# Routed attention and a PReLU layer on one core: sums of a pair of heads in one product, inverses spread by one turn, checks by the batch, rows in other PSUM banks

## The chip, the cores and the metric

The kernel runs on one core of one Trainium2 chip. The metric is the device time of one execution in microseconds (us); a median of several runs is given. A core has the engines TensorE (PE; its weight loads are listed as PEld), VectorE (DVE), ScalarE (ACT), GpSimd (POOL) and SyncE (SP), each with a queue of its own; here SP, ACT and POOL issue DMA transfers.

## The reference

Two stages, one after the other. First, attention in which a query sees only the keys that were assigned to the same of 16 clusters:

```python
# q, k, v: (4, 8, 768, 64); centroids: (8, 16, 64)
q_assign = np.argmax(np.einsum('bhsd,hcd->bhsc', q_n, c_n), axis=-1)   # rows normed
k_assign = np.argmax(np.einsum('bhsd,hcd->bhsc', k_n, c_n), axis=-1)
mask = q_assign[:, :, :, None] == k_assign[:, :, None, :]
scores = np.where(mask, scale * np.matmul(q, k.transpose(0, 1, 3, 2)), -1000000000.0)
attn = np.exp(scores - np.max(scores, axis=-1, keepdims=True))
attn = attn / (np.sum(attn, axis=-1, keepdims=True) + 1e-09)
x = np.matmul(attn, v)                 # then (B,H,S,D) -> (B*S, H*D) = (3072, 512)
...
h = x @ w_in                           # w_in (512, 2048)
g = np.maximum(h, 0.0) + alpha * np.minimum(h, 0.0)
return (g @ w_out).astype(np.float32)  # w_out (2048, 512)
```

`w_in`, `w_out` and `alpha` come in as words of 64-bit floats and are turned into 32-bit ones on the way.

## The kernel before, in words

**Tiles and steps.** Heads are worked in pairs: 4 batches x 4 pairs give 16 pairs n = 0 to 15 (`pairs`, L104). For the first three batches (n < NO = 12) a pair's 768 queries go in two halves of 384 against all six key chunks of 128, three steps of two chunks each: 72 steps. I call these far blocks. The last batch (n = 12 to 15) is sorted: the tokens of each head are put into the order of their clusters in HBM (`order_*`, L472 to L682), so that a key chunk has to meet only its neighbours (`window`, L694). Such a near block also has three steps, 72 to 83 in all, and makes both halves ("sides") of a pair at once.

**What a block does.** `score` multiplies keys by queries and takes exp on ScalarE; `mask` zeroes (VectorE, L772) what belongs to another cluster; `add_up` or `add_near` adds the chunks for the denominators, `turn` transposes 32 x 32 blocks (L801), `rows_sums` reduces them (L807), `total` adds over partitions by a product with the constant `fold` (L817), `invert` takes reciprocals and spreads them over a 128 x 384 tile `rd` by transposes (L827, L832), `weigh` or `weigh_near` makes the products with v (L861, L897), and `normalise` multiplies them with `rd` (L965, L903). The first batch's first half sums by products with ones instead (L854 to L882). After each inverse, `check` (L326) takes the lowest and highest of its words for a flag that is read at the end.

**Last batch.** Its result has to go back to the old order. `normalise_near` writes `outT`; `to_rows` (L923) transposes three chunks at a time on TensorE into PSUM and ScalarE copies them (L930); `put_back` scatters rows to HBM by 12 indirect DMAs on POOL (L935); `fetch_back` loads them on SP (L947), and `turn_back` transposes them on VectorE into the FFN's input xT (L957).

**FFN.** `ffn_pieces` cuts the FFN of half a batch into 28 pieces: `hidden(f)` (8 matmul records, L989, a ScalarE copy, L995, and a VectorE operation for the slope a piece later, L981) and `final` (8 records, L1007; every second one ends with a copy or addition of y, L1013 and L1015, and the last with a store). They fill PE between the steps.

**The order is written out by hand.** From step 24 on, a block of three steps has 12 slots (2 + 5 + 5, counted here 0 to 11). In each slot, `tick` first runs what was put off (`later(k, ...)`: k ticks on), then one entry of `todo` (masks, additions, turn, sums, product), one of `sorting`, then `feed` lets a number of FFN pieces go, spread evenly over the 48 slots of four blocks; `kept(block)` says how many are held back at their end (10 for the last four blocks, whose pieces fill the tail while the rows return). Then come the preparations of later blocks (`prep_at`). In the tail (L1228) two ticks and one piece alternate. In near blocks the product of side 0 is entry 6 of `todo`, its inverse entry 7, the product of side 1 entry 11.

**Buffers in PSUM.** `ps_m` (tile `mps`, from `misc()`) has one buffer, used for cluster similarities, clusters, `total`, rows and the products of side 1 in near blocks. `ps_f` (tile `fps`) has two that go round, used for FFN pieces and for one chunk of each `score`. `ps_s` and `ps_v` hold scores and weighted sums.

Of the kernel before, what the change touches and what calls it, by code (L numbers as in the profile page):

```python
# [23 lines left out]
def kernel(  # L24
# [122 lines left out]
    alf = const.tile([NF, P], FP32, name="alf")  # L147
# [54 lines left out]
    cn = const.tile([P, D], FP32, name="cn")  # L202
# [119 lines left out]
    lowest = const.tile([P, 2 * NP], FP32, name="lowest")  # L322
    highest = const.tile([P, 2 * NP], FP32, name="highest")
    WORDS = [float((127 + e) * 2 ** 23) for e in (-50, 40)]

    def check(n, half, inverses):  # L326
        i = 2 * n + half
        for to, op in ((lowest, ALU.min), (highest, ALU.max)):
            nc.vector.tensor_reduce(out=to[:, i:i + 1], in_=inverses.bitcast(I32), axis=AX.X,
                                    op=op)  # L330
# [157 lines left out]
    def order_constants():  # L488
        ordc = sorts["ordc"]
        stage = [ordc.tile([P, NX // PARTS, P], FP32, name=f"stage{i}") for i in range(STAGES)]  # L490
        for t in stage:
            nc.gpsimd.memset(t, 0.0)
# [9 lines left out]
        brief = asg.tile([P, HS], FP32, name="simT")  # L502
        for i, pattern in enumerate(kinds):
            row = (ordc.tile([P, P], FP32, name=f"row{i}") if i else brief[:, 0:P])
            nc.gpsimd.iota(row, pattern=pattern, base=0, channel_multiplier=0,
                           allow_small_or_imprecise_dtypes=True)
            own = brief[:, P:2 * P]
            nc.gpsimd.tensor_tensor(out=own, in0=row, in1=ident, op=ALU.mult)
            nc.vector.tensor_reduce(out=cols[:, i:i + 1], in_=own, axis=AX.X, op=ALU.add)
            rows.append(row)  # L510
        same = brief[:, 2 * P:3 * P]
        nc.vector.tensor_scalar(out=same, in0=rows[1], scalar1=cols[:, 1:2], scalar2=None,
                                op0=ALU.is_equal)


        before, within = rows[1], rows[2]
        nc.vector.scalar_tensor_tensor(out=before, in0=rows[0], scalar=cols[:, 0:1],
                                       in1=same, op0=ALU.is_gt, op1=ALU.mult)
        nc.vector.scalar_tensor_tensor(out=same, in0=rows[0], scalar=cols[:, 0:1],
                                       in1=same, op0=ALU.is_equal, op1=ALU.mult)  # L520
        nc.vector.scalar_tensor_tensor(out=within, in0=rows[2], scalar=cols[:, 2:3],
                                       in1=same, op0=ALU.is_gt, op1=ALU.mult)
        nc.vector.tensor_tensor(out=within, in0=within, in1=before, op=ALU.add)


        shift = ordc.tile([P, 2], FP32, name="shift")
        nc.vector.tensor_scalar(out=shift[:, 0:1], in0=cols[:, 2:3], scalar1=-float(HS),
                                scalar2=None, op0=ALU.mult)
        nc.vector.tensor_scalar(out=shift[:, 1:2], in0=cols[:, 1:2], scalar1=2.0,
                                scalar2=float(S), op0=ALU.is_ge, op1=ALU.mult)  # L530
        nc.vector.tensor_scalar(out=shift[:, 1:2], in0=shift[:, 1:2], scalar1=-1.0,
                                scalar2=None, op0=ALU.add)
# [20 lines left out]
    def order_counts(n, ps):  # L553
# [11 lines left out]
        for i, piece in enumerate(pieces):  # L565
            later(i, piece) if i else piece()
# [238 lines left out]
    def rows_sums(n, half):  # L805
        part = rdp.tile([P, 2 * NX], FP32, name="part")
        nc.vector.tensor_reduce(out=part, in_=accTs.pop((n, half)), axis=AX.X, op=ALU.add)  # L807
        parts[n, half] = part
# [4 lines left out]
    def total(n, half):  # L813

        if (n, half) in parts:
            ps = misc()
            nc.tensor.matmul(out=ps[:, 0:2 * NX], lhsT=fold, rhs=parts.pop((n, half)),  # L817
                             start=True, stop=True)
            totals[n, half] = ps

    def invert(n, half):

        if (n, half) not in totals:
            return
        ps = totals.pop((n, half))
        inv = rdp.tile([P, 2 * NX], FP32, name="inv")
        nc.vector.reciprocal(out=inv, in_=ps[:, 0:2 * NX])  # L827
        pool = sorts["ordp"] if n >= NO and half else rdp
        rd = pool.tile([P, HS], FP32, name="rd")
        for h in range(2):  # L830
            r = slice(h * D, (h + 1) * D)
            nc.vector.transpose(  # L832
                out=rd[r, :],
                in_=inv[r, h * NX:(h + 1) * NX, None].broadcast_to((D, NX, Q)))
        rds[n, half] = rd
        check(n, half, inv)

    def weigh(m, denominators=False):
# [24 lines left out]
        if denominators and done:  # L863
# [6 lines left out]
            inv = rdp.tile([P, 2 * NX], FP32, name="inv")  # L870
# [5 lines left out]
            for h in range(2):  # L876
                nc.vector.tensor_copy(out=inv[h * D + Q:(h + 1) * D, 0:NX],
                                      in_=inv[h * D:h * D + Q, 0:NX])
            rd = rdp.tile([P, HS], FP32, name="rd")
            nc.vector.transpose(out=rd, in_=inv[:, 0:NX, None].broadcast_to((P, NX, Q)))  # L880
            rds[n, half] = rd
            later(1, lambda: check(n, half, inv[:, 0:NX]))  # L882
# [17 lines left out]
    def normalise_near(n):  # L900
# [13 lines left out]

        starts = (4, 6) if n == NP - 1 else (6, 10)
# [7 lines left out]
    def to_rows(outT, rows, i):  # L923

        ps = misc()
# [521 lines left out]
```

## Time and profile before

| | |
|---|---|
| median of 3 runs | 1000.96 us (1000.15 to 1003.37) |
| the profiled execution | 1003.53 us, span 1001.4 us |
| granted TensorE clock | 0.995 of full speed |
| PE busy | 968.5 us, 97% of the span |
| DVE, ACT, POOL busy | 650.4, 259.6, 211.8 us |
| L989, L1007 (FFN products) | 342.9 and 339.2 us of PE |
| L772 (masks) / L832 (spreading inverses) / L329 (checks) | 131 us / 32.1 us (56 of 573 ns) / 10.9 us (64 instructions) |

The profile is one execution on the chip. Busy times overlap between engines. A wait is put down to the instruction that released it; times of a timeline row are its start and its duration, with the idle time of its engine before it in brackets. Matmul ends are modelled, and the next one may start 0.17 us before the end shown of the one ahead of it.

### The profile page before, as it was taken

The numbers are of one execution on the slowest core, as the hardware profiler recorded it, in microseconds if no ns is written. First come the engines' busy times: TensorE is split into PE (matmuls) and PEld (weight loads), VectorE is DVE, ScalarE is ACT, GpSimd is POOL, SyncE is SP. The second block draws the span as 40 slices with busy tenths as digits, with TensorE's granted clock in tenths as the row PEclk, the third lists the DMA queues.
The fourth block names the chain that finished last, engine by engine and source line by source line (L and its number), as shares of the span: only waits on it lengthen the run. The fifth ranks groups of instructions, "written<-read, shape, count | busy, mean of one in ns | idle before, by whom it ended". The sixth has DMA issues, their size and how long they took to land.

```text
span 1001.4 us, 10929 instructions
## 1 busy us (share of the span) xinstructions
PE 968.5 (97%) x3955; PEld 482.1 (48%) x3955; DVE 650.4 (65%) x1209; ACT 259.6 (26%) x468; POOL 211.8 (21%) x249
## 2 busy tenths in 40 slices
PE   8899999989999999999999999999988999999997
PEld 5434444445454454545445454454544545455453
DVE  5887788598487776877868698687987523021010
ACT  5655443223122221312222022231222101110110
POOL 2323222000000644301000263620044540000000
PEclk9989999999999999999999999999999999999999
DMA  6533553032100252415010121710521020000000
GB/s 248 199 108 108 137 135 71 16 67 44 32 1 21 87 114 56 84 40 106 1 32 0 53 80 34 148 35 17 85 60 31 24 50 22 0 5 29 0 1 34
DMA packets 174286, 60.46 MB, mean 60 GB/s; under 512 B 161216, under 2 KB 164752, under 8 KB 174224
## 3 DMA queue, kind: packets, MB, share of 16 engines
q1 hardware_dynamic: 168768, 51.42, 21.7%
q0 software_dynamic: 4608, 7.87, 2.3%
q8 instruction: 33, 0.54, 0.2%
q10 hardware_dynamic: 848, 0.39, 0.2%
q14 instruction: 29, 0.24, 0.1%
HBM read 45.15 MB, written 14.16 MB: 59 GB/s over the span
## 4 chain that ended last, share of the span: by engine, by line
PE 87%; DVE 8%; ACT 2%; issue 1%; DMA 1%; ACTq 0%; POOL 0%; DVEq 0%; POOLq 0%
PE fps L1007 31%; PE fps L989 31%; PE vps L861 8%; PE sps L731 7%; PE fps L731 3%; PE sps L740 1%; PE vps L897 1%; PE mps L371 1%; DVE gT L981 1%; DVE more L772 1%; PE mps L897 1%; DVE acc L801 1%; ACT E L752 1%; ACT member L416 1%; DMA aq<-member 1%
## 5 line engine op out<-in xcount | busy, mean ns | idle before, releaser
L989 PE MATMUL fps<-xT,w_in_sb 128*128 128x384 f32 x1024 | 342.9, 490 | 1.8 <-DVE y L1015 1.8
L1007 PE MATMUL fps<-w_out_sb,gT 128*128 128x512 f32 x768 | 339.2, 596 | 2.1 <-DVE gT L981 1.1
L989 PEld LDWEIGHTS fps<-xT,w_in_sb 128*128 128x128 f32 x1024 | 190.8, 190 | 140.5 <-issue 5.2
L1007 PEld LDWEIGHTS fps<-w_out_sb,gT 128*128 128x128 f32 x768 | 143.5, 190 | 173.9 <-issue 162.1
L637 POOL DMA_INDIRECT scratch<-stage,off x96 | 101.7, 1059 | 333.9 <-DMA stage<-in_v_dram 275.3
L981 DVE SCALAR_TENSOR_TENSOR gT<-gT,alpha 128x384 f32<-128x384 f32 x128 | 80.5, 635 | 133.8 <-ACT gT L995 127.1
L995 ACT COPY gT<-fps 128x384 f32<-128x384 f32 x128 | 61.3, 479 | 337.3 <-PE fps L989 328.4
L731 PE MATMUL sps<-qkT 64*128 64x384 f32 (+1 forms) x512 | 97.8, 501 | 0.7 <-ACT E L752 0.7
L772 DVE SCALAR_TENSOR_TENSOR more<-aq,key,more 128x384 f32<-128x384 bf16 (+1 forms) x136 | 74.5, 604 | 27.4 <-ACT more L752 14.0
L752 ACT ACTIVATE E<-sps 128x768 f32<-128x768 f32 (+1 forms) x81 | 61.2, 802 | 74.0 <-PE sps L740 45.8
L935 POOL DMA_INDIRECT back<-rows,place x48 | 48.7, 1015 | 108.9 <-ACT rows L930 95.2
L731 PEld LDWEIGHTS sps<-qkT 64*128 64x128 f32 x512 | 46.3, 189 | 45.2 <-issue 16.8
L861 PE MATMUL vps<-E,vt 128*64 128x384 f32 x356 | 67.0, 502 | 0.0
L1015 DVE TENSOR_TENSOR y<-y,fps 128x512 f32<-128x512 f32 x30 | 20.5, 683 | 67.3 <-PE fps L1007 67.3
L772 DVE SCALAR_TENSOR_TENSOR E<-aq,key,E 128x384 f32<-128x384 bf16 (+1 forms) x104 | 56.6, 601 | 8.3 <-ACT E L749 3.9
L782 DVE TENSOR_TENSOR acc<-acc,E 128x768 f32<-128x768 f32 x47 | 44.9, 955 | 16.7 <-ACT E L752 15.4
L1013 ACT COPY y<-fps 128x512 f32<-128x512 f32 x24 | 14.1, 586 | 140.3 <-PE fps L1007 127.4
L752 ACT ACTIVATE more<-sps 128x768 f32<-128x768 f32 (+1 forms) x47 | 35.5, 796 | 38.7 <-PE fps L1007 21.6
L861 PEld LDWEIGHTS vps<-E,vt 128*64 128x64 f32 x356 | 23.3, 138 | 32.4 <-issue 32.1
L861 PE MATMUL vps<-more,vt 128*64 128x384 f32 x220 | 38.8, 491 | 0.0
L269 POOL TENSOR_TENSOR w_in_sb<-w_in_sb,power 128x512 f32<-128x512 f32 x16 | 22.2, 1387 | 70.9 <-DVE w_in_sb L266 70.9
L269 POOL TENSOR_TENSOR w_out_sb<-w_out_sb,power 128x512 f32<-128x512 f32 x16 | 23.5, 1473 | 52.9 <-DVE w_out_sb L266 52.9
(175 smaller groups left out, 741.1 us busy)
## 6 DMA issues: line engine op xcount, KB each, us to landing
raw<-in_moe_w_in_dram SPq DMA_DIRECT2D x16, 512.0 KB
raw<-in_moe_w_out_dram SPq DMA_DIRECT2D x16, 512.0 KB
out_dram<-y SPq DMA_DIRECT2D x24, 256.0 KB
vt<-in_v_dram SPq DMA_DIRECT2D x12, 384.0 KB
qk<-in_q_dram SPq DMA_DIRECT2D x48, 96.0 KB
qk<-in_k_dram SPq DMA_DIRECT2D x48, 96.0 KB
qk<-scratch SPq DMA_DIRECT2D x32, 96.0 KB
qk<-in_q_dram SPq DMA_DIRECT2D x4, 384.0 KB
```

The source lines that it names most:

```text
L269: nc.gpsimd.tensor_tensor(out=dst, in0=dst, in1=power[0].bitcast(FP32), op=ALU.mult)
L637: nc.gpsimd.indirect_dma_start(out=scratch[n][1][h * NX + xx], out_offset=bass.IndirectOffsetOnAxis(ap=ranks[n][:, xx, h:h + 1], axis=0), ...
L731: nc.tensor.matmul(out=bank(ps, h, m), lhsT=qkT[r:r + D, S + c * P:S + (c + 1) * P], rhs=qkT[r:r + D, tokens], start=True, stop=not early_ ...
L752: nc.scalar.activation(out=E[:, :, 0:m], in_=ps[:, :, 0:m], func=AF.Exp, scale=SCALE)
L772: nc.vector.scalar_tensor_tensor(out=e, in0=of, scalar=keys[n][:, NJ + c, h:h + 1], in1=e, op0=ALU.is_equal, op1=ALU.mult)
L782: nc.vector.tensor_tensor(out=acc, in0=acc if first is None else first[3], in1=E, op=ALU.add)
L861: nc.tensor.matmul(out=po[r:r + D, 0:HS], lhsT=vts[n][:, h, c, :], rhs=e[:, h, :], start=(c == 0), stop=(c == NJ - 1))
L935: nc.gpsimd.indirect_dma_start(out=to[i], out_offset=bass.IndirectOffsetOnAxis(ap=place[:, h, j:j + 1], axis=0), in_=rows[:, j, h * D:(h + ...
L981: nc.vector.scalar_tensor_tensor(out=gs[f], in0=gs[f], scalar=alpha[:, f:f + 1], in1=gs[f], op0=ALU.mult, op1=ALU.max)
L989: nc.tensor.matmul(out=ps[:, 0:HS], lhsT=w_in_sb[:, c, f * P:(f + 1) * P], rhs=xTs[b, half][:, c, :], start=(c == 0), stop=(c == NCH - 1))
L995: nc.scalar.copy(gs[f], ps[:, 0:HS])
L1007: nc.tensor.matmul(out=ps[:, 0:DM], lhsT=gs[f][:, i * P:(i + 1) * P], rhs=w_out_sb[:, f, :], start=on and f == f0, stop=off and f == f0 + ...
```

## The change

Five things, in the words of the code:

- **Sums.** `rows_sums` of a near block writes both sides into one tile (`parts`), and one `total` at the end of the block multiplies both by `fold`. The inverse of both sides is taken at the start of the next block (`invert(prior[0], 0, 1)`); the product of side 0 in the middle of the block and its inverse go.
- **Inverses.** They are kept in one constant tile `inverses` with eight places, one for each of a batch's pairs and halves. Each head's reciprocals are written on that head's own 64 partitions, so one transpose of 128 partitions spreads both heads (`spread_out`), where before two of 64 did. `check` for every inverse becomes `check_inverses` for a batch, when the first inverse of the next batch is due, and once at the end.
- **Order constants.** The POOL products go to three places of the still unused `stage` tile, with one reduction for all three (before: one each, through one buffer); the VectorE pieces are put off by 5 to 8 ticks.
- **Rows.** `to_rows` takes `ps_f` instead of `misc()`, and starts at 6 and 9 ticks (before 6 and 10, and 4 and 6 for the last pair). The last four blocks keep 12 FFN pieces instead of 10.
- **Slots.** Clusters of later pairs are made in slot 0 of their step (before 2), the block transposes of a near pair one step later and in slots 0 and 1, and the last two pieces of the count for the order two ticks later. The tile `alf` (slopes as read) shares the place of `top`, `cn` that of `inverses`.

```diff
-    alf = const.tile([NF, P], FP32, name="alf")
+    alf = asg.tile([P, 2 * HS // Q, NC], BF16, name="top").rearrange(
+        "p t c -> p (t c)").bitcast(FP32)[0:NF, 0:P]
...
+    kept_of = [0]
+
+    def inverse(n, half):
+
+        if pairs[n][0] > kept_of[0]:
+            check_inverses()
+        return inverses[:, (2 * n + half) % (2 * NCH), :]
+
+    def check_inverses():
+        i = kept_of[0]
+        kept_of[0] += 1
+        words = inverses.bitcast(I32).rearrange("p n x -> p (n x)")
         for to, op in ((lowest, ALU.min), (highest, ALU.max)):
-            nc.vector.tensor_reduce(out=to[:, i:i + 1], in_=inverses.bitcast(I32), axis=AX.X,
-                                    op=op)
+            nc.vector.tensor_reduce(out=to[:, i:i + 1], in_=words, axis=AX.X, op=op)
...
+        own = stage[0][:, 0:len(kinds), :]
         for i, pattern in enumerate(kinds):
...
-            own = brief[:, P:2 * P]
-            nc.gpsimd.tensor_tensor(out=own, in0=row, in1=ident, op=ALU.mult)
-            nc.vector.tensor_reduce(out=cols[:, i:i + 1], in_=own, axis=AX.X, op=ALU.add)
+            nc.gpsimd.tensor_tensor(out=own[:, i, :], in0=row, in1=ident, op=ALU.mult)
...
+        def columns():
+            nc.vector.tensor_reduce(out=cols, in_=own, axis=AX.X, op=ALU.add)
+            for t in stage:
+                nc.gpsimd.memset(t, 0.0)
...
+        for i, piece in enumerate((columns, sums_before, sums_within, shifts)):
+            later(5 + i, piece)
...
         for i, piece in enumerate(pieces):
-            later(i, piece) if i else piece()
+
+            later(i if i < len(pieces) - 2 else i + 2, piece) if i else piece()
...
     def rows_sums(n, half):
...
+        near = n >= NO
+        if not near or half == 0:
+            parts[n] = rdp.tile([P, 1 + near, 2, NX], FP32, name="parts" if near else "part")
+        nc.vector.tensor_reduce(
+            out=parts[n][:, half if near else 0].rearrange("p h x -> p (h x)"),
+            in_=accTs.pop((n, half)), axis=AX.X, op=ALU.add)
...
+    def invert(n, *halves):
...
+        invs = [inverse(n, half) for half in halves]
+        i = (2 * n + halves[0]) % (2 * NCH)
         for h in range(2):
             r = slice(h * D, (h + 1) * D)
-            nc.vector.transpose(
-                out=rd[r, :],
-                in_=inv[r, h * NX:(h + 1) * NX, None].broadcast_to((D, NX, Q)))
-        rds[n, half] = rd
-        check(n, half, inv)
+            nc.vector.reciprocal(out=inverses[r, i:i + len(halves), :], in_=ps[r, :, h, :])
+        for half, inv in zip(halves, invs):
+            spread_out(n, half, inv)
+
+    def spread_out(n, half, inv):
+        pool = sorts["ordp"] if n >= NO and half else rdp
+        rd = rds[n, half] = pool.tile([P, HS], FP32, name="rd")
+        nc.vector.transpose(out=rd, in_=inv[:, :, None].broadcast_to((P, NX, Q)))
...
-        starts = (4, 6) if n == NP - 1 else (6, 10)
+        starts = (6, 9)
...
-        ps = misc()
+        ps = ps_f.tile([P, 512], FP32, name="fps")
...
-            at(u - 4, FIRST, lambda n=n: prep_clusters(n))
+            at(u - 4, 0, lambda n=n: prep_clusters(n))
             for i in range(2):
-                at(u - 2, FIRST + i, lambda n=n, i=i: order_blocks(n, i))
+                at(u - 1, i, lambda n=n, i=i: order_blocks(n, i))
...
-                at(u - 4, FIRST, lambda n=n: prep_clusters(n))
+                at(u - 4, FIRST if u - 4 < TOGETHER else 0, lambda n=n: prep_clusters(n))
...
-        return {NS // UB - 2: 4, NS // UB - 1: 10}.get(block, 0)
+        return {NS // UB - 2: 4, NS // UB - 1: 12}.get(block, 0)
...
             if prior[1] is None:
-                invert(prior[0], 1)
+                invert(prior[0], 0, 1)
                 weigh_near()
...
-                         lambda n=n: (total(n, 0), turn(n, 1), rows_sums(n, 1)),
-                         lambda n=n: invert(n, 0)]
-                todo += [lambda: None] * 3 + [lambda n=n: total(n, 1)]
+                         lambda n=n: (turn(n, 1), rows_sums(n, 1))]
+                todo += [lambda: None] * 4 + [lambda n=n: total(n)]
```

## The prediction

> **What bounds the kernel now.** I read the busy table first, then the list of what TensorE waited for, then the timeline around each of those waits. Busy time:
>
> ```profile
> PE 968.5 (97%) x3955; PEld 482.1 (48%) x3955; DVE 650.4 (65%) x1209; ACT 259.6 (26%) x468; POOL 211.8 (21%) x249
> PE 87%; DVE 8%; ACT 2%; issue 1%; DMA 1%; ACTq 0%; POOL 0%; DVEq 0%; POOLq 0%
> ```
>
> TensorE (PE) is the bound: 97% busy, 87% of the chain that ended last. The change takes almost nothing from PE itself, so all it can win are PE's stalls. The whole list of PE's waits (releaser; total us, times, longest us):
>
> ```profile
> PE fps L344 <- ACT qkT L348: 4.8, 2, 3.0
> PE mps L927 <- DVE inv L827: 4.2, 2, 2.7
> PE mps L817 <- DVE part L807: 3.9, 3, 1.7
> PE fps L989 <- DVE y L1015: 1.8, 1, 1.8
> PE mps L817 <- ACT every L433: 1.6, 3, 0.6
> PE mps L927 <- DVE qk L903: 1.2, 1, 1.2
> PE mps L927 <- ACT rows L930: 0.9, 1, 0.9
> PE mps L817 <- issue: 0.6, 1, 0.6
> ```
>
> Everything here with `mps` in it stands in line for one PSUM buffer (ps_m, bufs=1), which sums (L817), row transposes (L927), clusters (L429) and side 1 of the near products share. L344 and the waits left out (mostly L740, L1007, L200) belong to the first 80 us or to lines that the change does not touch. In time, the near blocks (steps 72 to 83, 684 to 792 us) show the pattern:
>
> ```profile
> 730.15 0.55 PE L927 MATMUL mps<-ident,qk 128*128 128x128 f32 x3 [2.68 <-DVE inv L827]
> 730.54 2.75 PE L989 MATMUL fps<-xT,w_in_sb 128*128 128x384 f32 x8
> 733.12 0.25 PE L429 MATMUL mps<-cluster,spread 128*128 128x24 bf16 x4
> 733.99 0.40 PE L817 MATMUL mps<-part,fold 128*128 128x24 f32 x2 [0.62 <-ACT every L433]
> ```
>
> The rows (L927) stand 2.68 us because `mps` holds the sums of side 0 until VectorE inverts them. The last thing to see is ScalarE in the tail:
>
> ```profile
> 798.84 0.48 ACT L995 COPY gT<-fps 128x384 f32<-128x384 f32 x1 [6.59 <-PE fps L989]
> 802.53 0.48 ACT L995 COPY gT<-fps 128x384 f32<-128x384 f32 x1 [3.21 <-PE fps L989]
> 802.91 0.48 ACT L930 COPY rows<-mps 128x384 f32<-128x384 f32 x1
> ```
>
> The rows were transposed at 799.37, but their copy (L930) is issued a slot later, behind the copy of the FFN tile fed in between (L995), so it starts at 802.91. This order decides my costs.
>
> **What the Trainium skill says.** "Perfetto Trace Analysis", Optimization Strategy: the same gap repeating on the engine that should be saturated can mean that PSUM is short for the next tile. The trace agrees: 11.8 us of the waits above are for `mps`-shaped tiles (4.2+3.9+1.6+1.2+0.9 us). "PSUM — Partial Sum Buffer", Engine vs sequencer instructions: the queues of ScalarE and VectorE are strict FIFO. The trace agrees: 802.91 above. "VectorE: DVE Perf Modes", The TRN2 errata: a VectorE operation pays a fixed latency per instruction, for an fp32 add (N+151)/0.96 ns; with N=384 an estimate of 557 ns, and L903 takes 547 to 558. For the reciprocal of 24 PSUM elements the page's 120+FD cycles would give 150 ns; the trace has 298, which I use.
>
> **The change, part by part.** Gains in us of the profiled span; "slot" is one of the 12 slots of a three-step block.
>
> 1. *Order constants.* Before, three POOL products and three VectorE reductions alternate in one buffer at 214 to 218 us; then ten VectorE operations (2.9 us by their rows of 0.15 to 0.35) run at once, the y addition is late and PE stands 1.85. Now one reduction and the rest go into slots 5 to 8 after. The same VectorE work (four reductions become one) then lies before the sums of its block. Without the POOL waits (about 1.3 us) they end about 228.4, PE comes to its sum at 229.2: hidden, by 0.8 us. The memsets of the stage move behind the reduction on POOL; POOL's first scatter is at 326 us. Gain **1.85** (0 to 1.85).
> 2. *Clusters at slot 0 instead of 2.* The sum follows five slots after the cluster instead of three, so the `every` copy (0.24) is long done. Gain 3 x 0.62 + 0.33 = **2.2**; the cost if ScalarE is late is the same wait again.
> 3. *The last two pieces of the order's count, two slots later.* L557 (0.49 start to start at 293.50) lay before turn and sums; PE then waited 1.07, twice. The scan already lay behind them. Gain 2 x 0.49 = **1.0** (0 to 2.1).
> 4. *Both sides in one product.* The sum of side 0 (four, 0.14 us of PE each: 724.51 to 724.65) goes: **0.6**. Its wait for sums of side 0 (1.75 at 751.05) goes. `mps` is no longer held for the inverse of side 0.
> 5. *Rows in ps_f, starts (6, 9).* The two waits for the inverse, 2.68 + 1.55, and the two in the tail, 1.25 + 0.95, go. Items 4 and 5 together without the 0.6: **8.2**.
> 6. *Inverses on a head's own partitions, batched checks.* Per far block before: reciprocal 0.30, two half transposes 1.16, two checks 0.35: 1.8. After: two reciprocals of 12 elements (between L873's 0.18 for 6 and 0.30 for 24; I take 0.22) and one transpose 0.58: 1.0. That is 0.8 x 20 = 16 us of VectorE (20 far inverses of this kind), plus some 4 us of checks elsewhere. On PE it is worth **0**: in far blocks VectorE next waits for the weighted sum (0.85 us at 241.00), so the time turns into idle time there. If it were on the path, up to 1 more. The near pair costs 2 x 0.30 + 1.15, as before. A batch check (two reductions of 96 elements, 0.25 each by L444) runs ahead of one inverse per batch: hidden by the same wait.
> 7. *The block transposes (L673) a step later*, behind the near sums: 1.8 us of VectorE off the path to the sum, nearer to the next score; that score comes 2.8 us after them by my count. They free the input buffers later, so SP's load of the last block's rows (L657, which stood 12.9 behind L673 once before) and the stores behind it wait until about 21 us into block 2; the rows are needed a block later, the stores by nobody. 0. The slopes' and centroids' new homes (`top`, `inverses`) are read before their owners write: 0.
>
> Sum of gains: 1.85+2.2+1.0+0.6+8.2 = **13.8**.
>
> What is **added**. I list which pieces fall where. Before, 22 FFN pieces go into the 48 near slots, after 20 (32 less the 12 kept), at slots 2, 4, 7, 9, 11. Rows come at slots 4 and 7, each with a piece right behind it in the same slot, and their ScalarE copy is issued a slot later, behind that piece's copy. ps_f has two buffers that go round, so:
> - the piece behind the rows takes the buffer of the piece before: it waits for that one's copy, 0.56 after its end less the rows' 0.16: 0.40. Blocks 2 and 3 and twice in the tail: 1.6.
> - the tile after that takes the rows' buffer, whose copy stands behind an FFN copy: 0.95, as seen at 802.49. Block 2 twice, block 3 once, tail once: 3.8.
> - block 4: the rows' copy stands behind a y copy (0.59): 1.0.
>
> Sum **6.4** (0 if the copies overtake, 8 if all waits are long). The four L927 pairs themselves move, not grow.
>
> The return of the rows: `turn_back` (L957) moves from slot 2 to slot 1 of the next block, while block 2 shrinks from 28.1 to about 24 us. POOL's 12 scatters take 1.27 each start to start (15.2), begin 14.7 us into block 2 (after the late copy), and the tail shows 6.1 us from the last scatter (818.75) to L957 (824.89). So the data is there 36 us after the start of block 2, 12 into block 3. VectorE arrives at 8.2 and stands about 3.8, with two masks, two near additions, turns and sums queued behind. Its sums then end at 22.6 into the block; PE reaches its sum at 21.7. Cost **0.9** (0 to 3.8). In block 4 the data arrives 6.4 in, before VectorE. SP waits in order for the scatters; only loads and stores with slack are behind it.
>
> The tail keeps 12 pieces instead of 10: about 6 us of FFN move from the near slots to the tail; the sum of PE work is unchanged. The return ends about 36 us into the tail, the 12 pieces at 43: cover 7 us, so 0.
>
> Net: 13.8 - 6.4 - 0.9 = **6.5 us**. The profiled execution took 1003.53 (span 1001.4 and 2.1 around it), so 997.0 for such an execution; it lies 2.6 above the median of the runs, so for the median 1000.96 - 6.5 = **994.5**.
>
> **Rivals.**
> - *The ps_f waits are shorter than I count*, as copies find their bank free. For it: PE has no such wait in its list today. Against: today rows are not in ps_f. Then 13.8 - 0.9, and each removed stall also returns the 0.17 by which the next matmul overlaps the end of the last: 11 x 0.17 = 1.9. Gain 14.8: 986.2.
> - *The gains are eaten*: the order constants keep their stall in other slots (1.85), L557 frees nothing, every rows tile waits 0.95 plus 0.40 (8 x 1.35 = 10.8). Then 13.8 - 1.85 - 1.0 - 10.8 - 0.9 = -0.8: about 1001.7, no change.
> - *Slower: VectorE stands at L957.* One in-order wait at slot 1 of blocks 3 and 4, price one us of PE per us that the return lands later than 11 into block 3 or 9 into block 4. For it: some scatters take 1.4 to 1.6, the slack is spent already. If it lands 6 us later than I count, block 3 costs 6.9 and block 4 3.8: 13.8 - 6.4 - 10.7 = -3.3, 1004.3; from there on it decides. Against: the SP queue issues promptly, and nothing slows POOL.
> - *It doesn't do what it says*: the first three items come, the near blocks stay as they are: 5.0 us, 996, inside my case.
>
> **How the numbers follow.** My case, a gain of 3 to 10.5 us (990.5 to 998): 0.58. More than that: 0.18. Between -3 and 3 us (about what a measurement of this kernel can tell from no change, 0.3%): 0.15. Slower: 0.09. Faster is 0.58 + 0.18 = 0.76. The range runs from 987.0, leaving out some 0.04 of the first rival, to 1000.5, leaving out 0.09 slower and 0.04 of the second.
>
> **What would show it.** Right: no PE wait on L807, on `every` or on inverses for the rows; the 1.85 at 221 us gone; new PE waits of 0.4 and 0.95 on ScalarE's FFN and rows copies after 705 us; one VectorE wait of 2 to 5 us on the DMA before L957 near 740. Wrong: PE idle in the near blocks above 12 us, waits of the first near scores for L673, or a VectorE wait before L957 beyond 8 us.

## The result, and the profile after

The changed kernel takes 996.78 us (median of 4 runs, 995.73 to 997.62) where the kernel before takes 1000.89 (1000.15 to 1003.37): a ratio of 0.9954, 95% interval 0.9934 to 0.9974. Profiled again beside the kernel before on another chip (the runs were spread over several) it took 997.06 against 1003.71, ratio 0.9929 (0.9916 to 0.9942). I predicted 994.5 in a range of 987.0 to 1000.5, and a gain of 6.5 us. The profiled executions gain 7.5 us of span in the first pair (1001.4 to 993.9) and 6.8 in the second (1002.1 to 995.3); the medians gain 4.1 and 6.6.

Two things have to be known to read differences this small. TensorE's granted clock is halved for stretches of 3.4 us, one to three times in an execution before its last microseconds, mostly before 75 us; each costs up to 1.7 us. So I compare from the start of step 24 (about 205 us) to the last product, and name a later stretch where one matters. And the profiles come in two kinds: those marked * in the table (the kernel before among them) show a few late wake-ups, places where ScalarE or VectorE starts microseconds after the product that it waits for has ended; the others do not. The last section has more on them.

The busy table and the line of the chain, as they answer to those of before:

```profile
PE 967.6 (97%) x3947; PEld 481.0 (48%) x3947; DVE 634.3 (64%) x1143; ACT 258.4 (26%) x468; POOL 211.4 (21%) x249
PE 89%; DVE 5%; ACT 2%; DMA 1%; issue 1%; POOL 0%; ACTq 0%; SPq 0%; DVEq 0%; POOLq 0%
```

VectorE lost 16.1 us of work (650.4 to 634.3), PE 0.9, and PE's busy time is still 97% of the span: what the change won is PE's waits. The list of these for the changed kernel (releaser; total us, times, longest us):

```profile
PE mps L845 <- DVE parts L832: 2.2, 1, 2.2
PE fps L1014 <- ACT gT L1020: 2.0, 6, 0.6
PE mps L845 <- DVE part L832: 1.6, 3, 0.6
...
PE fps L952 <- ACT gT L1020: 1.1, 2, 0.6
PE fps L1014 <- ACT y L1038: 0.7, 1, 0.7
```

L845 is the sums' product (L817 before), L832 the reduction ahead of it (L807), L952 the rows (L927), L1014 the hidden FFN product (L989), L1020 its copy. The prediction's near blocks 1 to 4 are those that start at steps 72, 75, 78 and 81; from here on a block is named by its first step. The rows' waits for `inv` (4.2) and for `qk` (1.2), the one for `every` (1.6) and the 1.8 behind L1015 are gone. New are the waits on `fps`, which are short and many, and one of 2.2 us for `parts`. In time, where the rows stood 2.68 us before:

```profile
712.80 0.49 PE L952 MATMUL fps<-ident,qk 128*128 128x128 f32 x3
713.53 2.85 PE L1014 MATMUL fps<-xT,w_in_sb 128*128 128x384 f32 x8 [0.24 <-ACT gT L1020]
716.41 0.48 ACT L1020 COPY gT<-fps 128x384 f32<-128x384 f32 x1 [2.94 <-PE fps L1014]
716.79 0.48 ACT L955 COPY rows<-fps 128x384 f32<-128x384 f32 x1
716.94 0.55 PE L952 MATMUL fps<-ident,qk 128*128 128x128 f32 x3 [0.57 <-ACT gT L1020]
...
720.74 2.85 PE L1014 MATMUL fps<-xT,w_in_sb 128*128 128x384 f32 x8 [0.48 <-ACT gT L1020]
```

The pattern is the one that the prediction drew: a piece follows the rows and waits for a bank, and the rows' copy (L955) stands behind the FFN's copy (L1020). But the second rows start at 716.94, released by the FFN's copy and 0.33 us before the rows' own copy has ended: they did not need the bank that this copy reads. They start 0.05 us after the copy of the piece between has ended (716.41 and 0.48 make 716.89). The long waits are 0.48 to 0.57, with one of 0.68 in block 81, not 0.95.

The other new wait is in block 78:

```profile
739.21 1.04 DVE L982 STREAM_TRANSPOSE xT<-qk 128x384 f32<-128x384 f32 x2 [4.74 <-DMA qk<-back]
...
746.84 1.98 PE L1032 MATMUL fps<-w_out_sb,gT 128*128 128x512 f32 x4 [0.44 <-DVE gT L1006]
...
751.03 0.42 PE L845 MATMUL mps<-parts,fold 128*128 128x48 f32 x2 [2.21 <-DVE parts L832]
```

VectorE stands 4.74 us at `turn_back` (L982, was L957) for rows that are still on their way back from HBM. Slopes and sums queue behind it, and PE stands 0.44 and 2.21 for them. That VectorE's queue is strictly FIFO is what the Trainium skill says ("PSUM — Partial Sum Buffer", Engine vs sequencer instructions); here it has a price.

The lengths of the blocks (score start to score start, us; columns * are of the second kind; the last three columns are kernels of the next section):

| steps | before* | after | before again* | after again* | turned rows later | product alone again* |
|---|---|---|---|---|---|---|
| 24 to 26 | 29.77 | 26.87 | 29.78 | 26.87 | 26.87 | 29.77 |
| 30 and 60 (each) | 26.29 | 25.82 | 26.28 | 25.82 | 25.82 | 26.28 |
| 66 | 27.95 | 26.09 | 28.00 | 27.16 | 26.09 | 27.99 |
| 69 | 26.58 | 26.75 | 26.58 | 26.75 | 26.75 | 26.58 |
| 75 | 28.11 | 23.66 | 28.11 | 23.66 | 23.66 | 24.99 |
| 78 | 28.73 | 32.00 | 28.74 | 32.20 | 28.82 | 27.33 |
| 81 and tail | 229.85 | 229.73 | 229.95 | 229.73 | 229.73 | 229.85 |
| step 24 to end | 790.62 | 783.52 | 790.77 | 784.80 | 780.36 | 785.93 |

Every block that is left out agrees within 0.2 us. The second pair (both marked *) differs by 5.97 from step 24 on, by 0.4 before it and by 0.5 after the last product, which is, but for rounding, the 6.8 of the spans.

### The profile page after: what moved, and what is told of

Read it like the earlier page. It is cut to its first block, busy times and chain, and to the rows that moved or that the text cites. A ratio compares the mean times of both kernels' runs of the same rounds, so it can differ in the third digit from the quotient of the medians.

```text
span 993.9 us, 10857 instructions
## 1 busy us (share of the span) xinstructions
PE 967.6 (97%) x3947; PEld 481.0 (48%) x3947; DVE 634.3 (64%) x1143; ACT 258.4 (26%) x468; POOL 211.4 (21%) x249
## 4 chain that ended last, share of the span: by engine, by line
PE 89%; DVE 5%; ACT 2%; DMA 1%; issue 1%; POOL 0%; ACTq 0%; SPq 0%; DVEq 0%; POOLq 0%
PE fps L1014 32%; PE fps L1032 32%; PE vps L890 9%; PE sps L754 8%; PE fps L754 3%; PE sps L763 1%; PE mps L381 1%; ACT E L775 1%; DMA aq<-member 1%; PE vps L923 1%; DVE acc L824 1%; ACT member L426 1%; PE mps L923 1%; DVE gT L1006 1%; PE vps L201 0%
## 5 line engine op out<-in xcount | busy, mean ns | idle before, releaser
L1014 PE MATMUL fps<-xT,w_in_sb 128*128 128x384 f32 x1024 | 343.5, 491 | 2.7 <-ACT gT L1020 2.0
L1014 PEld LDWEIGHTS fps<-xT,w_in_sb 128*128 128x128 f32 x1024 | 191.0, 190 | 142.5 <-ACT more L775 4.4
L1020 ACT COPY gT<-fps 128x384 f32<-128x384 f32 x128 | 61.2, 478 | 337.8 <-PE fps L1014 337.8
L754 PE MATMUL fps<-qkT 64*128 64x384 f32 x160 | 34.5, 509 | 0.0
```

Of the source, the lines that this page charges most:

```text
L754: nc.tensor.matmul(out=bank(ps, h, m), lhsT=qkT[r:r + D, S + c * P:S + (c + 1) * P], rhs=qkT[r:r + D, tokens], start=True, stop=not early_ ...
L1014: nc.tensor.matmul(out=ps[:, 0:HS], lhsT=w_in_sb[:, c, f * P:(f + 1) * P], rhs=xTs[b, half][:, c, :], start=(c == 0), stop=(c == NCH - 1))
L1020: nc.scalar.copy(gs[f], ps[:, 0:HS])
```

## The experiments

My theory was the prediction's: each gain is a PE wait that vanishes; the price is paid in `ps_f` banks and at `turn_back`. The rivals: VectorE's saved 16 us are what counts; the price lies in the bank of the rows; or the near blocks win from something else than the one product. The ratios below are to the kernel before, run beside each experiment. The changed kernel was run again beside experiments 9, 10 and 12 only, so in 1 to 8 the comparison with it is one profile against another, from step 24 on.

**1. Rows back in ps_m.** All else as changed.

```diff
-        ps = ps_f.tile([P, 512], FP32, name="fps")
+        ps = misc()
```

> The changed kernel, with the rows transposed into the one buffer of ps_m again. My theory: the single product already frees ps_m, so the waits of the rows for the inverse (4.2 us before) stay away; the nine waits in ps_f (3.8 us in all) go, and two waits of about 0.95 us for the rows' own copy come in blocks 2 and 3. Span 1 to 2 us below the changed kernel's 993.9, about 992.5. Rival: the other bank is what took the waits away; then 3 to 4 us of waits for ps_m come back and the span is about 997.

994.45 us against 1002.2, ratio 0.9934 (0.9922 to 0.9945); 781.68 us from step 24 on, 1.84 less than the changed kernel. Its waits:

```profile
PE mps L845 <- DVE parts L832: 2.3, 1, 2.3
PE mps L952 <- ACT rows L955: 1.9, 2, 1.0
...
PE mps L439 <- ACT rows L955: 0.9, 1, 0.9
```

In `ps_m` the rows cost three waits of 0.95 in the near blocks, one of 0.61 for sums behind them, and none in the tail: four waits, 3.5 us together. In `ps_f` there are nine, 3.8 us together, four of them in block 81 and the tail, and each wait costs more than its length (last section). So the move of the rows to other banks is not what helps: with one product for both sides, `mps` is free in time. The move costs 1.8 us, all of it after step 81 (227.79 against 229.73).

**2. The turned rows four slots later.**

```diff
-        later(4, turn_back)
+        later(8, turn_back)
```

> The changed kernel, with the transposes of the returned rows put off by 8 ticks instead of 4. My theory: VectorE's wait of 4.7 us on the returning DMA in block 3 delays its sums, and PE's 2.2 us at the product there plus 0.4 us at a slope are its price; both go, span about 991.3. Rival: VectorE's own work in that block is as long as PE's, and PE waits at the product as before: span within 0.5 us of 993.9.

992.54 us against 1002.2, ratio 0.9912 (0.9897 to 0.9926); 780.36 us from step 24 on, 3.16 less than the changed kernel. All of it is in block 78 (28.82 for 32.00). The same two places in its timeline:

```profile
740.98 1.03 DVE L982 STREAM_TRANSPOSE xT<-qk 128x384 f32<-128x384 f32 x2
...
747.42 0.32 PE L845 MATMUL mps<-parts,fold 128*128 128x48 f32 x2
```

No bracket stands behind either: VectorE reaches L982 when the rows are there, and PE's wait of 2.21 is gone, the 0.44 with it. The wait at `turn_back` cost PE 2.65 us plus the overlaps that come back, not 0.9.

**3. The order constants as before**: one buffer for three products, one reduction after each, the other operations at once.

```diff
-        own = stage[0][:, 0:len(kinds), :]
...
-            nc.gpsimd.tensor_tensor(out=own[:, i, :], in0=row, in1=ident, op=ALU.mult)
+            own = brief[:, P:2 * P]
+            nc.gpsimd.tensor_tensor(out=own, in0=row, in1=ident, op=ALU.mult)
+            nc.vector.tensor_reduce(out=cols[:, i:i + 1], in_=own, axis=AX.X, op=ALU.add)
...
```

> The changed kernel, with the order constants made as before, at once and through one buffer. My theory: PE's wait of 1.85 us near 219 us comes back and nothing else changes: span about 995.8. Rival: the spread pieces cost elsewhere as much as they save: span within 0.5 us of 993.9.

998.02 us against 1002.2, ratio 0.9964 (0.9950 to 0.9978). The block from step 24 on is 28.58 us long against 26.87: 1.71 more. The wait is back, behind the late addition of y (L1028 in this kernel; 1.85 behind L1015 in the kernel before):

```profile
222.22 5.43 PE L1002 MATMUL fps<-xT,w_in_sb 128*128 128x384 f32 x16 [1.44 <-DVE y L1028]
```

The whole stretch is 786.93, of which some 1.7 belong to one more stretch of half clock at 753.7; without it 785.2. Item 1 is confirmed at its size, 1.71 for 1.85.

**4. VectorE's savings given back.** Two half transposes for one, and two reductions per inverse into a tile that nothing reads; the batch check stays.

```diff
-        nc.vector.transpose(out=rd, in_=inv[:, :, None].broadcast_to((P, NX, Q)))
+        for h in range(2):
+            r = slice(h * D, (h + 1) * D)
+            nc.vector.transpose(out=rd[r, :], in_=inv[r, :, None].broadcast_to((D, NX, Q)))
+        words = inv.bitcast(I32)
+        for i, op in enumerate((ALU.min, ALU.max)):
+            nc.vector.tensor_reduce(out=cs_each[:, i:i + 1], in_=words, axis=AX.X, op=op)
```

> The changed kernel, where each inverse is spread by two transposes of 64 partitions and checked by two reductions of its own (into a tile that nobody reads), as well as by the batch: VectorE gets some 20 us more work. My theory: that is worth nothing on PE, span within 0.7 us of 993.9. Rival: VectorE's relief is part of the gain, and the span rises by 2 us or more.

999.12 us (997.80 to 1001.41, 15 runs) against 1002.2, ratio 0.9978 (0.9970 to 0.9986). The total speaks for the rival, its place does not. From step 24 on it takes 783.80 us, 0.28 more than the changed kernel. Between about 205 and 660 us VectorE works 12.6 us more (window; busy us and instructions of PE, PEld, DVE, ACT, POOL), first this kernel, then the changed one:

```profile
205.00:660.00 455.00, 453.01 (x1730) 223.46 (x1732) 356.34 (x653) 107.60 (x203) 112.85 (x128) 1.00 0.29 57
```

```profile
204.50:660.00 455.50, 454.28 (x1741) 224.20 (x1741) 343.76 (x604) 109.32 (x207) 111.95 (x128) 1.00 0.29 57
```

and no block there is longer. The cost lies before step 24: that step starts at 207.79 us, 2.9 later than in experiment 1, whose profile has the same two stretches of half clock. All of this grows before 107 us; VectorE converts the weights in that time too, but goes on with it to 176 us, so that alone is not the reason. So the far inverses' work is worth nothing from step 24 on, as predicted, and the VectorE work given back has a price only in the first 107 us. That price isn't the change's gain: the kernel before does the same half transposes and checks there and starts step 24 just 0.4 us after the changed kernel (205.42 and 205.03 in experiments 10 and 11). Why they cost more in this kernel than in the one before stays open.

**5. Ten pieces kept for the tail, not twelve.**

```diff
-        return {NS // UB - 2: 4, NS // UB - 1: 12}.get(block, 0)
+        return {NS // UB - 2: 4, NS // UB - 1: 10}.get(block, 0)
```

> The changed kernel, with 10 pieces of the FFN held back for the tail instead of 12. My theory: the tail had 7 us of cover to spare (the rows are back 36 us in, the pieces end at 43), so it stands without a wait; the near blocks get two more pieces, block 2 is longer and VectorE's wait for the returning rows in block 3 shrinks, and half of the rows come in slots without a piece: 4 us less than the changed kernel from step 24 on (783.5 there), span about 990. Rival: the 12 are needed, PE waits 2 us or more for the last rows, and the sum is no better than the changed kernel's.

995.82 us against 1004.84, ratio 0.9912 (0.9898 to 0.9925), but 783.84 us from step 24 on: 0.96 less than the profile of the changed kernel of its own kind (784.80). The wait for the sums in block 78 (1.38 in that profile) is gone: two more pieces lie ahead of it, VectorE finds the rows landed, and PE does not wait for them in the tail. Block 78 is 4.4 shorter and block 75 2.2 longer; some 2.6 of both is one FFN piece that has moved from the first to the second (block 75 has 48 records of L1014 for 40, block 78 has 8 for 16). The rest is 1.3 longer, 0.5 of it in waits for banks (0.35 at 772.45, 0.57 at 779.06 among them). That is less than I expected: fewer kept pieces hide the late rows, but most of the gain is lost in block 81 and the tail again, and where the remaining 0.8 us went I did not find.

**6. Rows at slots that have no piece behind them.**

```diff
-        starts = (6, 9)
+        starts = (5, 8)
...
-        later(4, turn_back)
+        later(5, turn_back)
```

> The changed kernel, with the rows transposed at 5 and 8 ticks instead of 6 and 9, in slots 3 and 6, where no piece of the FFN stands behind them (the end of the return is kept at 18 ticks). My theory: the rows' copy is then issued ahead of the next piece's copy on ScalarE; the waits of about 0.5 us go, those of 0.24 stay, and the rows land 3.5 us earlier, so VectorE waits some 2.3 us instead of 4.7 for them in block 3. From step 24 on about 779.3 (783.5 for the changed kernel), span about 990. Rival: the place does not matter, as the copy takes its turn anyway: span within 1 us of 993.9.

997.59 us (994.73 to 1000.54) against 1004.84, ratio 0.9923 (0.9909 to 0.9937). The waits of 0.57 and 0.48 in block 75 are gone and it shrinks to 22.63 as meant, but the whole stretch takes 788.28. A wait that nothing in the edit explains, and with it 6.8 us of half clock at 732.7, took more than the edit gave:

```profile
732.80 0.48 ACT L1020 COPY gT<-fps 128x384 f32<-128x384 f32 x1 [6.64 <-remote]
733.33 1.64 PE L754 MATMUL fps<-qkT 64*128 64x384 f32 x2 [4.49 <-ACT gT L1020]
```

The FFN product that this copy reads had ended at 726.92. A miss; what the edit itself is worth stays open. Experiments 10 and 11 come back to such waits.

**7. Rows in ps_m, at 5 and 8 ticks, the turned rows as late as in experiment 2.** Edits 1 and 6 together, with `later(9, turn_back)`.

> The changed kernel with three edits: rows in ps_m again, at 5 and 8 ticks, and their return taken up by VectorE at 22 ticks instead of 18. My theory: each removes what its run alone removed, and what ps_m cost (three waits of 0.95 us) goes as well: from step 24 on about 776.5, span about 986. Rival: VectorE bounds the near blocks once these waits are gone, and PE waits for sums again: above 779.

995.74 us (991.70 to 996.47) against 1004.84, ratio 0.9903 (0.9885 to 0.9921); 780.54 us from step 24 on. Less than the changed kernel's 784.80 of the same kind, but short of the sum, and on the side of the rival (above 779). Its waits for sums are there too, 0.65 and 0.67 us; more went to a late copy (PE stands 1.92 us at 727.56), which neither of the two foresaw.

**8 and 12. The one product alone.** The kernel before, with both sides' sums in one tile, one product, and both inverses at the next block's start; the inverses and checks themselves as before. Run twice.

```diff
-            nc.tensor.matmul(out=ps[:, 0:2 * NX], lhsT=fold, rhs=parts.pop((n, half)),
-                             start=True, stop=True)
+            nc.tensor.matmul(out=ps[:, 0:m * 2 * NX], lhsT=fold,
+                             rhs=part.rearrange("p s x -> p (s x)"), start=True, stop=True)
...
+                invert(prior[0], 0)
...
-                         lambda n=n: (total(n, 0), turn(n, 1), rows_sums(n, 1)),
-                         lambda n=n: invert(n, 0)]
+                         lambda n=n: (turn(n, 1), rows_sums(n, 1))]
...
```

> The kernel before, with one part of the change alone: both sides' sums in one product and both inverses at the start of the next block (rows, slots, order constants, checks and the number held back as before). My theory: the waits of 1.75, 2.68 and 1.55 us and four products go, 6.6 us: from step 24 on about 784.0 (790.6 before, 783.5 for the whole change). Rival: without the other bank the rows still stand for ps_m, and less than half of that comes.

> The kernel before with the one product and both inverses at the next block's start, and nothing else of the change, profiled once more: its first profile had gaps of 1.03, 0.75 and 1.46 us that no order of its own explains. My theory: without such gaps it takes about 784 us from step 24 to the end, the 786.4 measured less about 2.5; the waits of 1.75, 2.68 and 1.55 us of the kernel before are gone and the 0.95 us at the last block's rows stays. Rival: the gaps are this kernel's own (the two inverses meet the reloaded rows on VectorE), they return, and the stretch takes 786.4 us again.

999.23 against 1004.84, ratio 0.9944 (0.9930 to 0.9958), and 999.38 against 1003.71, 0.9953 (0.9941 to 0.9966); from step 24 on 786.43 and 785.93. The waits of 1.75, 2.68 and 1.55 of the kernel before are gone, with the rows still in `ps_m`: 4.8 of the 790.77 us. PE's whole list of waits from 700 to 800 us in experiment 12 (L932 is the rows, L821 the sums, L902 the products with v) shows none of the three; the 1.0 is the rows waiting for their own copy, as in the kernel before:

```profile
PE mps L902 <- DVE highest L329: 1.5, 1, 1.5
PE mps L932 <- ACT rows L935: 1.0, 1, 1.0
PE mps L902 <- issue: 0.8, 2, 0.4
PE fps L731 <- ACT more L749: 0.8, 1, 0.8
PE mps L821 <- ACT gT L1000: 0.6, 1, 0.6
```

The first rival (less than half of 6.6 us without the other bank) fell with that. My expectation of 784 failed both times, and the second rival was right on one place: a wait of 1.46 us that came back to the hundredth. It is this kernel's own, behind the last block's sums:

```profile
788.25 0.30 DVE L832 RECIPROCAL inv<-mps 128x24 f32<-128x24 f32 x1
788.58 1.16 DVE L837 STREAM_TRANSPOSE rd<-inv 64x384 f32<-64x384 f32 x2
...
790.05 0.31 DVE L832 RECIPROCAL inv<-mps 128x24 f32<-128x24 f32 x1
...
790.50 1.30 PE L902 MATMUL mps<-more,vt 128*64 128x384 f32 x8 [1.46 <-DVE highest L329]
```

The product of side 1 needs the bank of the sums, and VectorE frees it only with its second reciprocal, which stands behind the transposes and the two checks of the first side. The changed kernel takes both sides' reciprocals first, and its product of side 1 follows side 0's without a wait. But it also keeps twelve pieces, not ten, and its reciprocals start 1.64 us before the product of side 0 (778.13 and 779.77), here 1.16 us after that product has started (787.09). Experiment 5 parts the two: it keeps ten pieces and has the reciprocals first, they start 1.15 us into the product (786.36 and 785.21), and the product of side 1 starts 0.36 us after the last part of side 0's (786.77 and 787.13), where it takes 1.85 here (788.65 and 790.50). So with ten pieces kept the new form of the inverses is worth 1.5 us at this place. With twelve, an estimate from the durations above has the old form ready in time too, at 780.2 for a product that starts at 781.54; no run shows it. The other gaps near 740 (0.43, 0.39 and 0.75; 1.03 and 0.75 the first time) returned in size, but at a late exp; whether they are the kernel's own stays open.

**9. Both edits that paid**, the rows in `ps_m` and `later(8, turn_back)`.

> Both of the edits that paid alone, in one kernel: the rows' transposes in the banks of ps_m again, and the turned rows eight slots after their start in place of four. My theory: the two waits have nothing in common (the rows' copies hand back a bank of ps_f; VectorE waits for reloaded rows), so the gains add: from step 24 to the end 783.5 of the changed kernel, less 1.8, less 3.2, is about 778.5 us, and the time about 990.7 us where the kernel before runs 1002.2, a ratio of 0.9885. Rival: the three waits of 0.95 us that the rows have in ps_m return once nothing later covers them, and the pair is no better than the turned rows alone: 780.4 us from step 24 on, ratio 0.991.

993.59 us against 1003.71, ratio 0.9900 (0.9887 to 0.9913): on the same chip 3.5 us below the changed kernel's 997.06, and 3.75 less from step 24 on (781.05 against 784.80), where the sum of the two was 5.0. The tail has all of edit 1's gain (227.85). In block 78 the twelve scores from 733.3 on take 3.42 us where they take 1.92 in experiment 2, behind a late exp of the kind of experiment 6; without these 1.5 us the sum would hold. The rival's three waits of 0.95 us are there (at 718.08, 722.15 and 743.47), as in experiment 1, whose gain of 1.84 is what is left after them; and the interval holds the rival's ratio of 0.991, not my 0.9885. The interval overlaps those of experiments 2 and 7, so the three cannot be ranked.

**10 and 11. The kernel before, and the changed one, profiled again.** No edit.

> The kernel before, profiled once more. In its first profile two stretches of PE's gaps had no releaser in the kernel's own order (1.01 us at 637.79 and part of the 1.25 us at 798.12), each where PE's semaphore updates stood still for some 5 us. My theory: these belong to the execution and not to the program. They move or vanish, and from step 24 to the end the kernel takes 790.6 less at most 2.3, about 788.5 us, so that some 5 us, not 7, of the first comparison of profiles is the change. Rival: they belong to the order of instructions, return in the same places, and the stretch takes 790.6 us again.

> The changed kernel itself, profiled once more on the chip of this call, as the measure for the pair. My theory: the waits that the prediction is about return to within 0.1 us (0.24, 0.57 and 0.48 at the rows, 0.44 and 2.2 at the turned rows), and from step 24 to the end it takes 783.5 us; what else is found is the execution's own. The rival says that gaps such as the 4.5 us of the kernel with the rows off the pieces can open anywhere in any of these kernels; then up to two such gaps are seen here, and the stretch takes up to 789 us.

The kernel before took 1004.75 us (ratio to its own other runs 1.0003, 0.9996 to 1.0011) and 790.77 us from step 24 on. My theory that its gaps move or vanish fell: block 66 is 28.00 again, and 1.35 us stand at 798.64. (A stretch of half clock at 753.9 made the FFN products there 1.70 us longer, 5.38 for 3.68, and so used up the wait of 1.55 us behind them: block 78 is 28.74 for 28.73.) The changed kernel took 997.06 us and 784.80: its waits at the rows returned (0.24, 0.57, 0.48). At the turned rows VectorE stood 2.49 us instead of 4.74, and PE 1.38 for 2.21, with no 0.44. But block 66 took 27.16 instead of 26.09, and one exp woke late, first in this profile, then in the first one:

```profile
733.43 1.18 PE L754 MATMUL fps<-qkT 64*128 64x384 f32 x4
...
736.55 0.87 ACT L772 ACTIVATE more<-fps 128x384 f32<-128x384 f32 x2 [5.43 <-PE sps L754]
```

```profile
731.85 0.92 PE L754 MATMUL fps<-qkT 64*128 64x384 f32 x4
...
732.79 0.87 ACT L772 ACTIVATE more<-fps 128x384 f32<-128x384 f32 x2 [3.44 <-PE fps L754]
```

The same program: the exp starts 0.94 us after the start of its scores in one and 3.12 in the other. So the late wake-ups depend on the execution and not on the order of instructions alone, though among the profiles marked * they return in the same places. For the changed kernel they are some 1.3 us of the stretch. Hence the first pair of profiles compared unlike kinds, and I take 6.8, not 7.5, for the change.

## Why the prediction was right, step by step

- **Item 1, order constants, 1.85:** right. Putting them back costs 1.71.
- **Item 2, clusters at slot 0, 2.2:** right as far as the traces show; no run puts it back alone. The four waits are gone; block 24 is 1.19 shorter even with the order constants as before (28.58 in experiment 3 for 29.77), block 66 gives 0.84 on like profiles, and one new wait of 0.43 at 673.62, for `part`, takes some back in block 69 (+0.17).
- **Item 3, count pieces, 1.0:** right, by the traces alone too. Blocks 30 and 60 are 0.46 shorter each, 36 and 54 0.06: 1.04. A wait of 0.61 is left in two blocks; I had counted 0.58 left.
- **Items 4 and 5, 8.2 + 0.6:** the waits went, but my cause was half wrong. I put the gain down to both "rows in ps_f" and the one product. The one product alone takes the 2.68, 1.75 and 1.55 away; the move to `ps_f` costs 1.8 us net. The two waits in the tail stay away with the rows in `ps_m` as well (experiment 1), so they are not the gain of `ps_f` either; the 1.25 there was in part a late wake-up: the VectorE operation that the rows need (L903) started at 798.75, when the product that it reads had ended at 795.34. The reading behind this, 11.8 us of waits for `mps` as a shortage of PSUM, was too broad: the 3.9 of them behind L807 were waits for the sums themselves, and more banks do not shorten those.
- **Item 6, inverses, 0 on PE:** right from step 24 on in the far blocks (12.6 us of VectorE put back, no block longer). VectorE lost 16.1 us in all where I had counted some 20. After the last near block two reciprocals ahead of the transposes save PE 1.5 us if ten pieces are kept (experiments 5 and 12); I had not seen that.
- **Item 7, later block transposes, 0:** no new wait of a near score for them in the first profile.
- **Cost of ps_f, 6.4: too high, measured 3.8** (4 x 0.24, 3 x 0.57, 0.48, 0.68). The count of waits was near (nine for nine), their size was not. "The tile after that takes the rows' buffer" failed: the second rows start before the first rows' copy has ended, at the end of the copy of the piece between them. The 0.40 was 0.24, and the 0.95 was 0.57 or 0.48.
- **Cost of turn_back, 0.9: too low.** VectorE stood 4.74, not 3.8, and PE 2.65, not 0.9: 0.94 of the difference is VectorE's longer wait, for data that came 0.9 us later than counted, and 0.8 is slack: my 3.8 and 0.9 left 2.9 us between the two, 2.1 were there. Block 75 took 23.66 where I had counted about 24.
- **The tail, 0:** right. The 12 pieces cover the return.
- **The signs named ahead:** the wait of VectorE near 740 came, inside its 2 to 5 us, and the 1.85 at 221 is gone. The new waits on ScalarE came at other sizes. "No PE wait on L807" did not hold: two of 0.61 stayed, as item 3 itself had left them, and 0.43 and 2.21 were new.

The two mis-sized costs err against each other (2.6 too much, 1.75 too little), which leaves the net near 6.5: right in sign and in most of the mechanism (not in what `ps_f` is for), and close in size partly by that luck. The medians gain 4.1 and 6.6.

The rival "slower" named the right place, VectorE standing at L957. Its price, one us of PE per us of lateness beyond a slack, goes with the 4.74 and 2.65 of the first profile; in experiment 11 VectorE stood 2.49 and PE 1.38, so the slack is not the same in every execution. The data landed 0.9 us later than counted and not 6.

## What to carry to other kernels

An in-order engine must not be sent to data that may still be in flight: four slots more before one transpose were worth 3.2 us, nearly half of what the whole change won. When a bank is held too long, first ask who holds it and make that release earlier (one product for two sums, reciprocals ahead of the transposes); moving its waiting neighbour to a shared ring of two banks made nine short waits out of four. And what an engine's saved time is worth differs by stage: the VectorE work given back in experiment 4 cost 0.3 us after step 24 and 2.9 before it, for a reason that was not found.

## What the runs showed of the hardware

- A wait that vanishes returns more than its length. The next matmul record starts 0.17 us before the modelled end of the one ahead; and the first record of an FFN product after a wait is followed by its second 0.43 us later, where the others follow at 0.32. Together that is 0.27 us for each wait of such a product: experiment 3 has a wait of 1.44, and its block is 1.71 longer. Block 24 lost 2.90 us for waits of 1.85 + 0.62.
- In nine of the fourteen profiles, those of the kernel before and of experiments 5 to 12, PE's finished work reached ScalarE and VectorE up to 5.9 us late at some places (the copy of 732.80 in experiment 6), without anything in the program between. These traces also hold fewer semaphore updates (7,402 to 7,810) than the other five (9,788 to 9,851). The four of experiments 1 to 4, all taken on one chip, are without; the eight of 5 to 12, taken on two others, are all with. Whether chip, recording or both do it, no run here settles.
- Stretches of half clock, 3.4 us long, come around 50 and 70 us in most profiles, around 753.8 in two, and once, at 732.7 in experiment 6, for 6.8 us at the end of the longest of these waits.
